# Delta-rule attention feeding an MLP: y and the new state as separate pieces, and a new written order

## The chip, the cores and the metric

The kernel runs on one core of a Trainium2 chip. The metric is the device time of one execution in microseconds, from the median of three runs. The core has a matrix engine (TensorE, PE in the profile; its weight loads stand as PEld), three engines for element-wise work (VectorE or DVE, ScalarE or ACT, GpSimd or POOL), and SyncE (SP), which issues most transfers. Each engine works through its own instructions in order and waits on semaphores for the others.

## The reference, cut to what matters

```python
def _attn_ref(q, k, v, beta):                    # (4, 8, 768, 48) each, beta (4, 8, 768)
    k_n = k / (np.linalg.norm(k, axis=-1, keepdims=True) + 1e-06)
    state = zeros((B, H, D, D)); y = zeros_like(q)
    for t in range(S):
        kt, vt, bt = k_n[:, :, t], v[:, :, t], beta[:, :, t, None]
        y[:, :, t] = einsum('bhd,bhde->bhe', q[:, :, t], state)
        v_old = einsum('bhde,bhd->bhe', state, kt)
        state = state + bt[:, :, :, None] * einsum('bhd,bhe->bhde', kt, vt - v_old)
    return y

x = y.transpose(0, 2, 1, 3).reshape(3072, 384)
h = x @ w_in                                     # (384, 2048)
g = h * np.tanh(softplus(h))
out = g @ w_out                                  # (2048, 384)
```

All values are 32-bit floats; the two weights come as 64-bit floats, read as pairs of 32-bit words.

## The kernel before, in words

The 768 time steps are cut into NS = 12 chunks of 64 (n below), and the 32 heads into two halves h of 8 pairs of heads. Within a chunk the recurrence is a triangular system. It is solved for two chunks at once (group g covers chunks 2g and 2g+1) by `early` (L1363): TensorE makes k·k products (`pg`), VectorE transposes them into `gt` (L1421), goes through some 30 dependent steps of a product `pr` (L1467) and a sum into `gt` (L1469), scales (L1471) and transposes back into `d` (L1489). Group 0 is split in halves that are put together by `merge`.

Per chunk and half TensorE then makes these small products, all in plain 32-bit float, which take two matmuls and two weight loads each: `s_a` (`ta`) and `s_b` (`tb`) apply the solve to the masked products, `s_gq` (`gq`) multiplies keys with the old state and the queries, `s_z` (`pz`) gives the corrected values, and `s_y` (L1713) gives both the transposed output y (`py`) and the new state (`ps`). In `s_y` a head's 48 state columns are written as a piece of 32 and one of 16, because the helper `new_state` lays four pieces next to each other in the array's columns (hh = 0 and 1, two pieces each). The evictions of `ps` and `py` are one deferred piece `out`, which also issues the next chunk's keys and queries (`load_k`, `load_q`) and copies the new state into `xx` on ScalarE (L1735), and the output into `x`, as a high part on ScalarE (L1740) and a low part on VectorE (L1741).

The MLP works on a chunk's 256 rows in 8 units fp of 256 hidden columns. `g1` (L1786) makes `h` from `x` (18 matmuls, two terms of high and low parts), ScalarE applies Mish into `e` (L1801) and rounds it into the high part of `g` (L1802), VectorE forms the low part (L1803), and `g2` (L1820) adds 12 matmuls into `acc`. `acc` has one pair of PSUM tiles for all chunks, copied out by ScalarE when a chunk's 8 units are in. The weights are turned from 64-bit into high and low parts in the first part of the run (`convert`, pieces `cv`, on VectorE, ScalarE, TensorE and transfers issued by GpSimd). `keep_warm` runs products of zeros while TensorE would have nothing else.

The order of all engines is written out by hand. Every piece of work is an event with a name; `put` gives it its place from the table TT (a number that sorts a priority queue), and work that a piece defers (`defer`) is an event of its own, named after it with `.0>1` and so on. An event whose `need` labels are not given yet is put back. A second table, SLOT, says which of a pool's buffers a tile gets. `tile.manual_schedule` keeps the order in which the code then issues instructions on all five engines.

The lines that the change and the prediction touch:

```python
        def new_state():                                             # in s_y
            for p in range(PB):
                for hh in (1, 0):
                    for e, m in ((0, 32), (32, D - 32)):
                        r0 = 64 * (1 - hh) + e
                        yield ps[r0:r0 + m, p, :], x[:, p, hh, D + C + e:D + C + e + m], x[:, p, hh, 0:D]
```

Of the kernel before, what the change touches and what calls it, by code (L numbers as in the profile page):

```python
# [10 lines left out]
F32 = mybir.dt.float32  # L11
# [4 lines left out]
ALU = mybir.AluOpType  # L16
# [13 lines left out]
def bcast_in(ap, n):  # L30
# [18 lines left out]
    'loadv': [13],
    'turn_k(1,0).0>1': [14],  # L50
    'loado1': [15],
    'turn_k(0,0).0>1': [16],
    'early0': [17, 25, 27, 40, 49, 51, 52, 55, 58, 59, 61, 63, 64, 65, 68, 80, 82, 84, 92, 93, 96, 97, 100, 103, 104, 105, 107, 109, 110, 120, 121, 122, 125, 127, 129, 318, 482],
    'turn_k(0,1)': [18],
    'loadq': [19],
    'cv0': [20, 28, 31, 39, 117, 136, 144, 162, 1426],
    'turn_k(0,1).0>1': [21],
    'loadb': [22],
    'warm12.401': [24],
    'loado2': [26],  # L60
    'early0.0>1': [29],
    'warm43.6': [30],
    'loado0': [32],
    'early0.1>1': [33],
    'loado11': [34],
    'loado4': [35],
    'loadi4': [37],
    'turn_k(1,1).0>1': [38],
    'turn_beta()': [41],
    'warm36.4': [42],  # L70
    'early0.2>1': [43],
    'warm11.7': [44],
    'warm0.602': [45],
    'turn_q0(0,)': [47],
    'early0.3>1': [48],
    'cv3': [50, 149, 205, 209, 213, 237, 253, 269, 1263],
    'turn_q0(1,)': [53],
    'turn_q0(0,).0>1': [54],
    'scale_v(0,0)': [56],
    'turn_q0(0,).0>2': [57],  # L80
    'cv5': [60, 108, 145, 173, 197, 208, 225, 233, 1141],
    'warm11.501': [62],
    'warm29.5': [66],
    'warm11.6': [67],
    'warm11.602': [69],
# [48 lines left out]
    'loado8': [147],
# [1950 lines left out]
```

## Time and profile before

| what | value |
|---|---|
| median of 3 runs | 640.11 us (634.57 to 641.02) |
| the profiled execution's own time | 635.71 us |
| its span, first to last instruction | 634.0 us |
| TensorE busy | 601.8 us (95%), 11118 matmuls |
| TensorE weight loads busy | 557.0 us (88%), 11118 loads |
| VectorE busy | 381.3 us (60%) |
| ScalarE busy | 280.2 us (44%) |
| GpSimd busy | 79.7 us (13%) |
| mean granted clock of TensorE | 0.982 |
| moved by transfers | 43.39 MB, mean 68 GB/s |

The span is 1.7 us shorter than the execution's own time. Busy time is the union of an engine's instructions, so a TensorE that is busy need not be at its peak: small products overlap in the array. A group's "idle before" is the time for which its engine did nothing just before an instruction of the group, with what ended the idle time; "issue" means that the engine waited for nothing that the profile shows. [...]

### The profile page before, as it was taken

To read this page: it belongs to the slowest core of one execution; us is meant where nothing else is said; L and a number is where in the kernel's file an instruction comes from. 1 tells how busy PE (TensorE), PEld (TensorE's weight loads), DVE (VectorE), ACT (ScalarE), POOL (GpSimd) and SP (SyncE) were. 2 spreads that over 40 slices of the span, in tenths; PEclk is the share of its full clock that TensorE was granted. 3 is DMA by queue.
4 is the path that set the end of the run, shared out by engine and by line. 5 is a ranking of instruction groups with operands and counts; after the bars stand their busy time and mean duration, and the time that the engine had idled before them with its cause. 6 is when DMAs were issued, how large, how long until landed. Compare 5 with 4: busy or idle time off the path is not lost.

```text
span 634.0 us, 24961 instructions
## 1 busy us (share of the span) xinstructions
PE 601.8 (95%) x11118; PEld 557.0 (88%) x11118; DVE 381.3 (60%) x837; ACT 280.2 (44%) x531; POOL 79.7 (13%) x134
## 2 busy tenths in 40 slices
PE   7989879999999889999999998999999999999997
PEld 4546668899989789899998998999999999999996
DVE  3768778998696699965847745683653432321110
ACT  3338758645433354435342533443433344343231
POOL 5100223224100040000400020210030200000000
PEclk9899989999999989999999997999999999999999
DMA  9995567932433134214231213122112312010011
GB/s 190 309 321 124 95 128 123 164 51 53 61 53 65 23 52 61 50 18 74 53 59 28 53 23 56 41 38 51 29 26 53 52 28 44 9 27 1 1 26 25
DMA packets 161818, 43.39 MB, mean 68 GB/s; under 512 B 149008, under 2 KB 157712, under 8 KB 161712
## 3 DMA queue, kind: packets, MB, share of 16 engines
q1 hardware_dynamic: 156800, 37.12, 29.6%
q0 software_dynamic: 2736, 4.20, 4.0%
q8 instruction: 87, 1.43, 0.9%
q10 hardware_dynamic: 2176, 0.49, 0.4%
q14 instruction: 19, 0.16, 0.1%
HBM read 32.87 MB, written 4.72 MB: 59 GB/s over the span
## 4 chain that ended last, share of the span: by engine, by line
PE 74%; DVE 8%; DMA 7%; issue 4%; SPq 4%; ACT 2%; POOL 0%; DVEq 0%; POOLq 0%; ACTq 0%
PE acc L1820 27%; PE h L1786 26%; SPq L1206 4%; PE py L1599 4%; PE pz L1599 3%; PE gq L1599 3%; PE pg L1406 3%; PE ps L1599 2%; DMA wi<-mi 1%; DMA xx<-in_q_dram 1%; DVE g L1803 1%; DVE pr L1467 1%; DVE gt L1469 1%; DMA ri<-in_moe_w_in_dram 1%; PE warm L1846 1%
## 5 line engine op out<-in xcount | busy, mean ns | idle before, releaser
L1820 PE MATMUL acc<-wo,g 128*128 128x384 f32 x1152 | 218.3, 342 | 2.9 <-DVE g L1803 2.8
L1786 PE MATMUL h<-x,wi 128*128 128x256 f32 x1728 | 218.9, 283 | 1.3 <-DMA wi<-mi 1.0
L1786 PEld LDWEIGHTS h<-x,wi 128*128 128x128 f32 x1728 | 212.7, 190 | 3.3 <-DMA wi<-mi 1.2
L1820 PEld LDWEIGHTS acc<-wo,g 128*128 128x128 f32 x1152 | 199.3, 189 | 6.5 <-DVE g L1803 4.4
L1803 DVE TENSOR_TENSOR g<-e,g 128x512 fp32r<-128x512 f32 x96 | 67.7, 710 | 78.4 <-ACT g L1802 74.8
L1801 ACT ACTIVATE e<-h 128x512 f32<-128x512 f32 x96 | 57.2, 598 | 119.1 <-PE h L1786 72.8
L1802 ACT CAST g<-e 128x512 fp32r<-128x512 f32 x96 | 59.1, 620 | 74.8 <-PE acc L1820 72.7
L1469 DVE TENSOR_TENSOR gt<-gt,pr 128x58 f32<-128x58 f32 (+9 forms) x164 | 58.3, 355 | 4.0
L1467 DVE TENSOR_TENSOR pr<-gt 128x58 f32<-128x58 f32 (+9 forms) x164 | 57.4, 350 | 4.1
L1599 PE MATMUL gq<-xx,kt 48*64 48x112 f32 (+1 forms) x768 | 49.4, 270 | 0.7 <-DVE xx L1584 0.6
L1599 PEld LDWEIGHTS pz<-vt,tt 64*64 64x64 f32 x768 | 43.4, 135 | 5.2 <-issue 1.5
L1599 PE MATMUL pz<-vt,tt 64*64 64x48 f32 x768 | 47.1, 226 | 0.5 <-ACT tt L1664 0.4
L1599 PEld LDWEIGHTS gq<-xx,kt 48*64 48x64 f32 x768 | 44.1, 132 | 2.6 <-issue 1.5
L1584 DVE STREAM_TRANSPOSE xx<-xx 128x1024 f32<-128x1024 f32 x20 | 24.8, 1242 | 29.9 <-DMA xx<-in_q_dram 16.9
L1577 POOL TENSOR_TENSOR vt<-vt,ne 128x384 f32<-128x384 f32 x24 | 22.1, 927 | 147.0 <-DMA vt<-in_v_dram 73.7
L1688 DVE TENSOR_TENSOR xx<-gq,amask 64x256 f32<-64x256 f32 x96 | 40.1, 418 | 0.7
L1741 DVE TENSOR_TENSOR x<-py,x 128x384 fp32r<-128x384 f32 x24 | 13.3, 556 | 44.0 <-ACT x L1740 43.8
L1406 PE MATMUL pg<-kt 48*32 48x64 f32 x1536 | 29.3, 223 | 8.6 <-issue 6.9
L1508 POOL COPY tt<-d 32x512 f32<-32x512 f32 x40 | 26.8, 669 | 83.3 <-DVE d L1489 55.9
L1406 PEld LDWEIGHTS pg<-kt 48*32 48x32 f32 x1536 | 25.6, 111 | 13.1 <-issue 8.2
L1710 ACT COPY xx<-pz 64x384 f32<-64x384 f32 x48 | 22.8, 474 | 31.3 <-PE gq L1599 11.5
L1685 DVE TENSOR_TENSOR vt<-vt,gq 128x192 f32<-128x192 f32 x44 | 15.5, 352 | 26.1 <-PE gq L1599 17.2
(135 smaller groups left out, 577.2 us busy)
## 6 DMA issues: line engine op xcount, KB each, us to landing
ri<-in_moe_w_in_dram SPq DMA_DIRECT2D x24, 256.0 KB, 5.1
ro<-in_moe_w_out_dram SPq DMA_DIRECT2D x32, 192.0 KB, 4.9
kt<-in_k_dram SPq DMA_DIRECT2D x76, 64.0 KB, 2.7
vt<-in_v_dram SPq DMA_DIRECT2D x48, 96.0 KB, 3.1
xx<-in_k_dram SPq DMA_DIRECT2D x48, 96.0 KB, 3.2
out_dram<-o SPq DMA_DIRECT2D x48, 96.0 KB, 2.2
xx<-in_q_dram SPq DMA_DIRECT2D x80, 32.0 KB, 2.4
wo<-mo POOLq DMA_DIRECT2D x9, 192.0 KB, 4.1
```

What stands on the lines that cost most here:

```text
L1206: m = (nc.scalar if turns[0] else nc.sync).dma_start(out=dst, in_=src)
L1406: nc.tensor.matmul(ps[r0:r0 + 32, p8, :], kt[r, p, c, :], mv, start=True, stop=True)
L1467: nc.vector.tensor_tensor(out=pv, in0=nj, in1=xj, op=ALU.mult)
L1469: nc.vector.tensor_tensor(out=below, in0=below, in1=pv, op=ALU.add)
L1508: nc.gpsimd.tensor_copy(out=tt2[r, t2, :, c0:c0 + 32], in_=dts[g][r, t2])
L1599: last[:] = [nc.tensor.matmul(*a, start=True, stop=True)]
L1688: nc.vector.tensor_tensor(out=x[r, p4, hh, D:D + C], in0=ps[r, :, d:], in1=bcast_mid(amask[r], 4), op=ALU.mult)
L1786: nc.tensor.matmul(h[:, f2, :], wt["i", f * P // WI * NCH + c][:, i2, f0:f0 + P], x[:, c, :], start=(i == 0), stop=(i == 3 * NCH - 1))
L1801: for d, f in ((0.7, lambda: nc.scalar.activation(e, h, AF.Mish)), (0.7, lambda: nc.scalar.copy(out=gg[:, 0], in_=e)), (0.8, lambda: nc.ve ...
L1802: (0.7, lambda: nc.scalar.copy(out=gg[:, 0], in_=e)),
L1803: (0.8, lambda: nc.vector.tensor_tensor(out=gg[:, 1], in0=e, in1=gg[:, 0], op=ALU.subtract))):
L1820: nc.tensor.matmul(acc[t], gg[:, a, f2, ts_], wt["o", f][:, i2, :], start=(f == 0 and i == 0), stop=(f == NF - 1 and i == 2))
```

## The change

The new state is a stage of its own, `s_s`, with an event, an eviction and a PSUM tile of its own. Its products take all 48 columns of a head in one piece, so a chunk and half has 16 of them in place of 32. The keys of the next chunk are issued with the state's eviction, the queries with y's; the turned queries need y's eviction only (label R), the state's eviction gives label Y. An event of `s_s` stands behind each of `s_y`. Both tables are written anew: TT has other numbers for all events, SLOT other buffers. Two lines of TT as an example (y of chunk 2, half 0):

```diff
-    'ats_y[2,0]': [630],
-    'ats_y[2,0].0>1': [631],
+    'ats_y[2,0]': [639],
+    'ats_y[2,0].0>1': [640],
+    'ats_s[2,0]': [641],
```

The code:

```diff
@@ -1722,45 +1762,44 @@
         if n not in xs:
             xs[n] = [mp.tile([P, NCH, UT], F32R, tag=f"x{i}{n % 2}", name=f"x{i}_{n}", bufs=1) for i in range(2)]
         py = placed(pa, "pa", 4, [P, NCH, 2, C], F32, f"py{n}_{h}")
-        ps = placed(pa, "pa", 4, [P, PB, D], F32, f"ps{n}_{h}") if n < NS - 1 else None
-
-        def out():
-            def state():
-                if n < NS - 1:
-                    load_k(n + 1, h)
-                    if n:
-                        load_q(n + 1, h)
-                    for hh in range(2):
-                        r = slice(64 * (1 - hh), 64 * (1 - hh) + D)
-                        nc.scalar.copy(out=x[r, :, hh, 0:D], in_=ps[r])
-
-            def result():
-                hi, lo = (t[:, :, h * P:(h + 1) * P] for t in xs[n])
-                y = py.rearrange("r c q t -> r c (q t)")
-                nc.scalar.copy(out=hi, in_=y)
-                nc.vector.tensor_tensor(out=lo, in0=y, in1=hi, op=ALU.subtract)
-                give(f"X{n}.{h}")
-
-            for f in (result, state) if h or not n else (state, result):
-                f()
-
-        def turned_y(hh):
-            cols = lambda p, a, b: flat[:, (2 * p + hh) * W + a:(2 * p + hh) * W + b]
-            pieces = [(p, e, 32) for p in range(PB) for e in ((-16, 16) if p % 2 else (0,))] + [(p, 32, 16) for p in range(0, PB, 2)]
+
+        def result():
+            hi, lo = (t[:, :, h * P:(h + 1) * P] for t in xs[n])
+            y = py.rearrange("r c q t -> r c (q t)")
+            nc.scalar.copy(out=hi, in_=y)
+            nc.vector.tensor_tensor(out=lo, in0=y, in1=hi, op=ALU.subtract)
+            give(f"X{n}.{h}")
+            if 0 < n < NS - 1:
+                load_q(n + 1, h)
+
+        cols = lambda p, hh, a, b: flat[:, (2 * p + hh) * W + a:(2 * p + hh) * W + b]
+        pieces = [(p, e, 32) for p in range(PB) for e in ((-16, 16) if p % 2 else (0,))] + [(p, 32, 16) for p in range(0, PB, 2)]
+        todo = []
+        for hh in range(2):
             for p, e, m in pieces:
                 c, r0 = divmod(D * p + e, P)
-                yield py[r0:r0 + m, c, hh, :], cols(p, e, e + m), x[:, p, hh, D:D + C]
-
-        def new_state():
-            for p in range(PB):
-                for hh in (1, 0):
-                    for e, m in ((0, 32), (32, D - 32)):
-                        r0 = 64 * (1 - hh) + e
-                        yield ps[r0:r0 + m, p, :], x[:, p, hh, D + C + e:D + C + e + m], x[:, p, hh, 0:D]
-
-        todo = [*turned_y(0), *turned_y(1), *(new_state() if n < NS - 1 else ())]
+                todo.append((py[r0:r0 + m, c, hh, :], cols(p, hh, e, e + m), x[:, p, hh, D:D + C]))
         for i, a in enumerate(todo):
-            yield mm(*a, then=(lambda: defer(2.1, out, label=f"Y{n}{h}")) if i == len(todo) - 1 else None)
+            yield mm(*a, then=(lambda: defer(2.1, result, label=f"R{n}{h}")) if i == len(todo) - 1 else None)
+
+    def s_s(n, h):
+
+        x = xx[h]
+        ps = placed(pa, "pa", 4, [P, PB, D], F32, f"ps{n}_{h}")
+
+        def state():
+            load_k(n + 1, h)
+            for hh in range(2):
+                r = slice(64 * (1 - hh), 64 * (1 - hh) + D)
+                nc.scalar.copy(out=x[r, :, hh, 0:D], in_=ps[r])
+
+        todo = []
+        for p in range(PB):
+            for hh in (1, 0):
+                r0 = 64 * (1 - hh)
+                todo.append((ps[r0:r0 + D, p, :], x[:, p, hh, D + C:D + C + D], x[:, p, hh, 0:D]))
+        for i, a in enumerate(todo):
+            yield mm(*a, then=(lambda: defer(2.1, state, need=(f"y{n}{h}",), label=f"Y{n}{h}")) if i == len(todo) - 1 else None)
 
 
     def moe(n):
@@ -1918,9 +1957,10 @@
     asks = {s_a: lambda n, h=None: [f"d{n}.{i}" for i in range(2)] + ([f"M{n}.1" if n < 2 * FG else f"D{n}" if n % 2 else f"T{n // 2}"]),
             s_b: lambda n, h=None: [f"A{n}" if h is None else f"A{n}.{h}", f"N{n // 2}" if n >= 2 * FG else f"M{n}.1"], s_gq: Q,
             s_z: lambda n, h: [f"B{n}" if n else f"B{n}.{h}", f"V{n}{h}"] + ([f"D{n}"] if n >= 2 * FG else []) + [f"G{n}{h}{i}" for i in range(2 if n else 0)],
+            s_s: lambda n, h: ([f"U{h}", "x0"] if n == 0 else []) + [f"Z{n}{h}"],
             s_y: lambda n, h: ([f"U{h}", "x0"] if n == 0 else []) + [f"Z{n}{h}"] + [f"G{n}{h}{i}" for i in range(2)]}
 
-    took = {s_a: 1.2, s_b: 1.2, s_gq: 1.1, s_z: 1.1, s_y: 1.9}
+    took = {s_a: 1.2, s_b: 1.2, s_gq: 1.1, s_z: 1.1, s_y: 1.1, s_s: 0.9}
 
     def at(t, *stages):
         def run():
@@ -1928,7 +1968,7 @@
             tensor(sum(took[f] for f, _ in todo))
             together(*(f(*a) for f, a in todo))
             for f, a in todo:
-                if f in (s_z, s_y):
+                if f in (s_z, s_y, s_s):
                     give(f"{f.__name__[2]}{a[0]}{a[1]}")
 
         want = [x for f, *a in stages if a[0] < NS for x in asks[f](*a)]
@@ -1962,6 +2002,8 @@
             put("gq00", one(together, s_gq(0, h)), TN['gq0'][h], need=Q(0, h))
     for t, st in zip((TN['st'][0], *TN['st'][:2], *TN['st'][1:]), ((s_a, 0, 0), (s_a, 0, 1), (s_b, 0, 0), (s_b, 0, 1), (s_z, 0, 0), (s_z, 0, 1), (s_y, 0, 0), (s_y, 0, 1))):
         at(t, st)
+        if st[0] is s_y:
+            at(t, (s_s, *st[1:]))
 
     put(f"early{1}", early(1), *TN['e1'], *spread(us(1 + TN['s1'][0]), us(1 + TN['s1'][1]) + 10, 60), *(us(1 + TN['s1'][1]) + 11 + i for i in range(4)), need=("K2",))
 
@@ -2009,14 +2051,18 @@
         one_a, one_b = ([(f, n + 1)] * fused(n + 1) for f in (s_a, s_b))
         at(ts[0], (s_z, n, 0), (s_gq, n, 1), *one_a)
         at(ts[1], (s_y, n, 0))
+        if n < NS - 1:
+            at(ts[1], (s_s, n, 0))
         if n == 1:
             at(ts[2], (s_z, n, 1))
             at(us(TN['g20']), (s_gq, 2, 0))
         else:
             at(ts[2], (s_z, n, 1), (s_gq, n + 1, 0), *one_b)
         at(ts[3], (s_y, n, 1))
+        if n < NS - 1:
+            at(ts[3], (s_s, n, 1))
         for h, t in ((0, us(TN['c0'] if n == 1 else TN['g20'] if n == 2 else n - 2 + (TN['c2'] if n == 3 else TN['cc'])[2])), (1, ts[0])):
-            do(t - TN['tl'], turn_q, n, h, need=(f"L{n}{h}", f"Y{n - 1}{h}"))
+            do(t - TN['tl'], turn_q, n, h, need=(f"L{n}{h}", f"R{n - 1}{h}"))
             do(t - 5.0, scale_v, n, h, need=(f"P{n}", f"ne{n // 2}"))
     at(us(TN['ab'][0]), (s_a, 1))
     at(us(TN['ab'][1]), (s_b, 1))
```

What this does to TensorE's order is seen where products of y, of the state and of a later solve meet. Before, in the run of chunk 4's last MLP units (`acc_4`), the last state pieces of 32 and 16 columns are followed at once by the 64 `pg` products, then by `acc`:

```order
L1599 MATMUL ps_0_5893<-xx_104 32x48
L1599 MATMUL ps_0_5893<-xx_104 16x48
L1406 MATMUL pg_0_5963<-kt_5783 32x64 x32
L1406 MATMUL pg_1_5998<-kt_5783 32x64 x32
L1820 MATMUL acc_4_5580<-wo_2058,g_5_5476 128x384 x3
L1820 MATMUL acc_4_5580<-wo_2131,g_5_5476 128x384 x3
L1820 MATMUL acc_4_5581<-wo_2058,g_5_5476 128x384 x3
L1820 MATMUL acc_4_5581<-wo_2131,g_5_5476 128x384 x3
```

In the changed kernel the same half of a chunk ends with 16 state products of 48 columns, and an MLP product follows:

```order
L1639 MATMUL py_0_5706<-xx_104 32x64 x12
L1639 MATMUL py_0_5706<-xx_104 16x64 x4
L1639 MATMUL ps_0_5745<-xx_104 48x48 x16
L1825 MATMUL h_0_5762<-x_5_4965,wi_735 128x256
L1825 MATMUL h_0_5762<-x_5_4966,wi_735 128x256
```

and its `pg` products stand two MLP units later:

```order
L1859 MATMUL acc_4_5132<-wo_2359,g_6_5677 128x384 x3
L1859 MATMUL acc_4_5132<-wo_2265,g_6_5677 128x384 x3
L1859 MATMUL acc_4_5133<-wo_2359,g_6_5677 128x384 x3
L1859 MATMUL acc_4_5133<-wo_2265,g_6_5677 128x384 x3
L1446 MATMUL pg_0_5804<-kt_5626 32x64 x32
L1446 MATMUL pg_1_5837<-kt_5626 32x64 x32
L1825 MATMUL h_2_5874<-x_5_4965,wi_1206 128x256
```

The `pg` products have moved away from `py` and `ps`; MLP products with 2 instructions each stand between the small ones with 4.

On VectorE the end of the solve for chunks 4 and 5 is the second place. Before, the low part of chunk 3's output (`x_3`, from `py_1`) stands ahead of the last two instructions of the solve:

```order
L1467 TENSOR_TENSOR pr_30_3889<-gt_2779 128x30
L1469 TENSOR_TENSOR gt_2779<-gt_2779,pr_30_3889 128x30
L1741 TENSOR_TENSOR x_3_3573<-py_1_3904,x_3_3572 128x3x128
L1471 TENSOR_TENSOR gt_2779<-gt_2779,y_2783 128x1024
L1489 STREAM_TRANSPOSE d_1907<-gt_2779 128x32x32
L1685 TENSOR_TENSOR vt_0_3506<-vt_0_3506,gq_01_3867 128x192
```

Now the solve ends without it; that `x_3` comes right behind these rows:

```order
L1507 TENSOR_TENSOR pr_29_3805<-gt_2807 128x58
L1509 TENSOR_TENSOR gt_2807<-gt_2807,pr_29_3805 128x2x29
L1507 TENSOR_TENSOR pr_30_3808<-gt_2807 128x30
L1509 TENSOR_TENSOR gt_2807<-gt_2807,pr_30_3808 128x30
L1511 TENSOR_TENSOR gt_2807<-gt_2807,y_2811 128x1024
L1529 STREAM_TRANSPOSE d_1778<-gt_2807 128x32x32
L1770 TENSOR_TENSOR x_3_3417<-py_1_3771,x_3_3416 128x3x128
```

The instruction that needs TensorE's `py_1` has moved behind the transposition into `d`.

In the written order the start is another one, too. Chunk 0's keys are turned before chunk 1's, behind 19 products of zeros in place of 8, and beta is loaded first on ScalarE's queue; 12 of the zero products stand ahead of the product that turns beta. Queries and values of chunk 0 are loaded behind more of the weights.

## Rows read from the trace of the kernel before

**Rows 1.** The page, part 1: busy time of each engine, share of the span, instructions.

```profile
PE 601.8 (95%) x11118; PEld 557.0 (88%) x11118; DVE 381.3 (60%) x837; ACT 280.2 (44%) x531; POOL 79.7 (13%) x134
```

**Rows 2.** Groups of TensorE by line and shape, 76.7 to 634 us; columns as titled.

```profile
line engine op names shapes xcount | busy us, mean ns | idle before us <-releasers
...
L1406 PE MATMUL pg<-kt 48*32 48x64 f32 x1280 | 25.1, 225 | 7.0 <-issue 6.9
...
L1599 PE MATMUL ps<-xx 128*16 128x48 f32 x640 | 17.6, 206 | 0.2 <-issue 0.2
L1599 PE MATMUL ps<-xx 128*32 128x48 f32 x640 | 17.6, 206 | 3.5 <-issue 3.5
```

**Rows 3.** Windows cut inside the waits called issue; counts in brackets.

```profile
core 0: us, PE busy (x) PEld busy (x) DVE busy (x) ACT busy (x) POOL busy (x), PEclk, DMA share, GB/s
...
64.90:68.90 4.00, 3.13 (x127) 2.18 (x127) 3.89 (x10) 2.80 (x6) 0.00 (x0) 1.00 0.33 58
...
72.80:88.30 15.50, 12.16 (x379) 9.96 (x380) 12.24 (x26) 11.67 (x21) 4.34 (x6) 1.00 0.85 161
...
98.50:179.50 81.00, 77.52 (x1521) 73.10 (x1521) 70.05 (x158) 47.60 (x90) 20.50 (x31) 1.00 0.51 84
```

**Rows 4.** The page, part 3: the queue that brings instructions.

```profile
q8 instruction: 87, 1.43, 0.9%
```

**Rows 5.** Windows, each some 256 TensorE instructions long and ended by a wait.

```profile
176.16:179.70 3.54, 2.20 (x142) 1.96 (x132) 3.05 (x9) 2.28 (x6) 0.00 (x0) 1.00 0.22 42
...
382.41:386.66 4.25, 2.19 (x144) 1.95 (x132) 1.91 (x4) 0.00 (x0) 0.00 (x0) 0.95 0.52 96
```

**Rows 6.** Timeline of TensorE, 308.5 to 313 us: start, length, what.

```profile
308.64 1.10 PE L1599 MATMUL py<-xx 128*32 128x64 f32 x64
309.56 0.86 PE L1599 MATMUL ps<-xx 128*32 128x48 f32 x64
310.35 2.35 PE L1820 MATMUL acc<-wo,g 128*128 128x384 f32 x12
```

**Rows 7.** Timeline of TensorE, start-up: products of 64 columns, two abreast.

```profile
59.15 1.14 PE L1599 MATMUL pz<-vt,tt 64*64 64x48 f32 x32 [0.42 <-ACT tt L1664]
```

**Rows 8.** Windows with a lowered granted clock (column PEclk).

```profile
88.60:93.00 4.40, 4.40 (x32) 4.10 (x31) 2.76 (x6) 1.32 (x3) 0.00 (x0) 0.61 0.35 64
...
386.60:393.20 6.60, 6.55 (x111) 6.38 (x112) 3.33 (x5) 3.01 (x6) 0.00 (x0) 0.51 0.34 49
225.80:229.30 3.50, 3.50 (x27) 3.45 (x20) 2.98 (x3) 2.16 (x4) 0.83 (x2) 0.51 0.25 35
```

**Rows 9.** Timeline of VectorE, end of the solve for chunks 4 and 5.

```profile
219.97 0.56 DVE L1741 TENSOR_TENSOR x<-py,x 128x384 fp32r<-128x384 f32 x1 [4.65 <-ACT x L1740]
220.44 1.22 DVE L1471 TENSOR_TENSOR gt<-gt,y 128x1024 f32<-128x1024 f32 x1
221.70 1.98 DVE L1489 STREAM_TRANSPOSE d<-gt 128x1024 f32<-128x1024 f32 x1
```

**Rows 10.** Timeline of TensorE: the product that waits for it.

```profile
224.77 1.21 PE L1599 MATMUL ta<-d,at 32*32 32x32 f32 x64 [2.02 <-DVE xx L1688]
```

**Rows 11.** Windows: the solve for chunks 2 and 3.

```profile
99.40:146.30 46.90, 44.97 (x562) 42.36 (x560) 44.14 (x105) 29.07 (x55) 11.51 (x16) 1.00 0.65 105
```

**Rows 12.** The page, part 5: what lies between a first and a second MLP product.

```profile
L1803 DVE TENSOR_TENSOR g<-e,g 128x512 fp32r<-128x512 f32 x96 | 67.7, 710 | 78.4 <-ACT g L1802 74.8
L1801 ACT ACTIVATE e<-h 128x512 f32<-128x512 f32 x96 | 57.2, 598 | 119.1 <-PE h L1786 72.8
L1802 ACT CAST g<-e 128x512 fp32r<-128x512 f32 x96 | 59.1, 620 | 74.8 <-PE acc L1820 72.7
```

**Rows 13.** Timeline of TensorE: the first MLP product on TensorE.

```profile
76.70 2.37 PE L1786 MATMUL h<-x,wi 128*128 128x256 f32 x18
```

**Rows 14.** Timeline of VectorE, start-up.

```profile
20.86 0.36 DVE L1265 TENSOR_SCALAR ro<-ro 128x384 f32<-128x384 f32 x1 [2.48 <-DMA ro<-in_moe_w_out_dram]
```

**Rows 15.** Who waited for whom, total, times, longest.

```profile
DVE g L1803 <- ACT g L1802: 74.8, 31, 8.9
```

More of the change, by code (lines that the diff above doesn't have):

```diff
@@ L54 @@
[L54 to L73, printed above, removed]
@@ new lines @@
+    'merge0.2>1': [187],
+    'merge0.3>1': [190],
+    'ats_a[0,0]': [191],
+    'ats_a[0,0].0>1': [192],
+    'loado9': [193],
+    'ats_a[0,1]': [195],
+    'ats_a[0,1].0>1': [197],
+    'loado10': [200],
+    'merge1': [201, 229, 246, 286],
+    'cv22': [203, 204, 237, 262, 455, 480, 486, 487, 502],
+    'warm12.301': [205],
+    'warm40.201': [206],
+    'unit(0,)': [207],
+    'ats_b[0,0]': [211],
+    'ats_b[0,1]': [213],
+    'warm11.801': [214],
+    'cv15': [215, 219, 239, 346, 347, 348, 349, 354, 1227],
@@ new lines @@
+    'ats_gq[0,1].0>1': [217],
+    'cv13': [224, 315, 336, 367, 368, 369, 371, 381, 920],
+    'ats_b[0,0].0>1': [225],
+    'ats_b[0,1].0>1': [227],
+    'merge1.1>1': [230],
+    'merge1.0>1': [232],
+    'ats_z[0,0]': [233],
+    'ats_z[0,0].0>1': [234],
+    'ats_z[0,1]': [235],
+    'loadx': [236],
+    'cv21': [243, 301, 302, 340, 434, 460, 461, 462, 463],
+    'unit(1,)': [247],
+    'loadi5': [250],
+    'cv9': [251, 260, 261, 276, 284, 291, 292, 293, 438],
+    'loadp': [252],
+    'scale_v(1,0)': [253],
@@ new lines @@
+    'g1.2.0': [703],
+    'g1.2.0.0>1': [704],
+    'g1.2.1': [705],
+    'ats_y[3,0]': [706],
+    'g1.2.1.0>1': [707],
+    'g1.2.1.0>2': [708],
+    'early3.2>1': [709],
+    'ats_s[3,0]': [712],
+    'g2.1.7': [721],
+    'ats_y[3,0].0>1': [723],
+    'prep(4,)': [728],
+    'g2.1.7.0>1': [731],
+    'scale_v(4,1)': [732],
+    'g1.2.0.0>2': [733],
+    'g1.2.0.0>3': [734],
+    'g1.2.1.0>3': [739],
+    'g1.2.2': [740],
+    'g1.2.2.0>1': [741],
+    'turn_q(4,0)': [742],
+    'early3.6>1': [745],
@@ new lines @@
+    'g2.2.2': [782],
+    'g1.2.5': [784],
+    'g1.2.5.0>1': [786],
+    'g1.2.5.0>2': [787],
+    'g1.2.5.0>3': [788],
+    'ats_a[4].0>1': [789],
+    'g2.2.3': [790],
+    'g2.2.4': [791],
+    'turn_q(4,1)': [796],
+    'prep(5,)': [797],
+    'g1.2.6': [798],
+    'g1.2.6.0>1': [799],
+    'g1.2.7.0>2': [800],
+    'g1.2.7.0>3': [801],
+    'g1.2.6.0>2': [802],
+    'g1.2.6.0>3': [803],
+    'ats_b[4]': [804],
+    'ats_s[3,1]': [805],
+    'ats_b[4].0>1': [806],
+    'g1.3.1': [807],
+    'scale_v(5,0)': [808],
@@ L959 @@
+    'g2.11.6': [1592],
+    'g2.11.7': [1593],
+    'g2.11.7.0>1': [1594],
+    'g2.11.7.0>2': [1595],
 }
 SLOT = {
[72 rows of a table removed]
[68 rows of a table added]
 }
```

1688 lines of the change are left out of this document (813 added, 875 removed), and 187 rows, old and new, of tables (SLOT, TT).

## The prediction

> **What bounds the kernel now.** I read the page's first part first. TensorE is busy 601.8 us, 95% of the span; VectorE 60%, ScalarE 44% [rows 1]. So from the first MLP product at 76.7 us [rows 13] to the end the time is TensorE's work, its few pauses, and what a lowered clock costs. The groups of TensorE name the pauses: of all small products after 76.7 us, `pg` waited 7.0 us and `ps` 3.7 us, and nearly all of both, 6.9 + 3.5 + 0.2 = 10.6 us, is put down to "issue", a wait for nothing that the profile shows [rows 2].
>
> What is that wait? I cut windows at the places where it occurs and counted matmuls and weight loads between them: 254, 759 and 3042 [rows 3]. These are 1, 3 and 12 times 256, short by about 1%. The queue that brings instructions moved 1.43 MB in 87 packets, 16.4 KB each, and 87 times 256 is 22,272, against the 22,236 matmuls and loads that TensorE has [rows 1, 4]. So I read the pauses as TensorE waiting for its own instructions, which come in blocks of 256. The stretches that end in such a pause are short ones: about 270 instructions in 3.54 and 4.25 us, with 1.3 and 2.1 us of it idle [rows 5]. They are places where `py`, `ps` and `pg` stand back to back. A small fp32 product takes four instructions and little time: 64 `py` records and 64 `ps` records pass in 1.71 us, where 12 `acc` records alone take some 2.3 [rows 6].
>
> [...]
>
> **The change, part by part.** The sum starts from the profiled execution's own time, 635.7 us.
>
> *State products in pieces of 48 columns.* 64 records become 32 per chunk and half, 22 times. That is half the instructions, but not half the time: before, four pieces lie beside each other in the array, and 64 records pass in 0.79 us (`ps` at 309.56, `acc` at 310.35) [rows 6], 16 sets of four. The 32 new ones stand two abreast, again 16 sets, each with the same 48 columns to stream. I take the same time, 0. Bounds: half the time if instructions were what counts, -0.40 × 22 = -8.7. Above, the nearest row with two abreast: 32 records of `pz` last 1.14 us, 64 of `ps` 0.86 [rows 6, 7], +0.28 × 22 = +6.1. The two ends are far apart, and the middle is supported by streaming alone.
>
> Where `py` gives way to `ps` nothing pauses before: the two overlap in the records [rows 6]. [...]
>
> *Pauses for instructions.* Some 700 matmuls and as many loads go, and above all the written order no longer puts `pg` behind `py` and `ps`; MLP products stand between them, which give the queue time. A block of 256 took about 3.3 us to arrive when the engine outran it (3.54 us for 274 instructions in the first of rows 5). In the new order the runs of small products without MLP work between them are shorter than two blocks in all but a couple of places. -10.6, and I leave 1.5 for those: -9.1. Ends: -10.6 and 0.
>
> *Clock behind those pauses.* The first two stretches of rows 8 follow pauses of this kind. They cost (1 - 0.61) × 4.4 = 1.7 and (1 - 0.51) × 6.6 = 3.2 us. If the pause goes, so does the stretch: -4.9. Ends: -4.9 and 0.
>
> *The wait of `ta` for chunk 4.* In the new order the low part of `x` is behind the transposition, so the solve's end no longer waits for `py`: -2.0 [rows 10], and with it its clock stretch, (1 - 0.51) × 3.5 = -1.7 [rows 8]. What is late next is `ta` of chunk 2. VectorE is 44.14 of 46.90 us busy in that solve [rows 11]: what TensorE saves up to there it has to wait for, unless VectorE gains too, by 2.8 us at the most. I count +3 for that, ends 0 and +6.
>
> *Start-up.* The order of loads is new, and so are the 19 products of zeros. Up to 76.7 us one pause for instructions lies at 64.9 to 68.9, where TensorE is busy 3.13 of 4.00 us [rows 3], and VectorE waits 2.48 us for a weight's load [rows 14]. I take -2 for the first MLP product. Ends: both waits gone and as much again by an earlier solve, -6; a load that comes as late as that one does now, +2.5.
>
> *Evictions.* The state's ScalarE copies and `y`'s are now two events, and the keys of the next chunk are issued with the one, the queries with the other. The number of instructions on ScalarE and VectorE is the same, and both have idle time, so 0; the cover is ScalarE's 56% of idle time [rows 1].
>
> *New close neighbours.* Between the first and second MLP product of a unit stand 0.60, 0.62 and 0.71 us, 1.93 in all, without the handovers [rows 12]. In the new order a second product follows its first at about 2 us of TensorE's work in three places, and `acc` of one chunk follows the copy of the last one directly in two. Each may cost up to its 1.93 us less what stands between: +3 in all, ends 0 and 5 × 1.6 = +8.
>
> Sum: 635.7 + 0 - 9.1 - 4.9 - 2.0 - 1.7 + 3 - 2 + 3 = 622.0 us for an execution like the profiled one. That execution lies 4.4 us under the median of the runs, 640.1, and 1.1 above the fastest of them, 634.6. The mean of the four times that I have (634.6, 635.7, 640.1, 641.0) is 637.9, 2.1 above the profiled one. I add these 2 us and forecast 624, 2.5% under the median before. I take 1% as what a measurement can tell from no change here.
>
> For its own range I take the root of the squares of the terms' half widths, about 7.4 (state products), 5 (pauses), 2.5 (clock), 3 (VectorE), 4 (start-up) and 4 (neighbours): 11 us to either side, 613 to 635.
>
> **Rivals.**
>
> *The pauses stay.* The "issue" waits could be something else than instructions on their way, or the blocks could fall as badly in the new order. For it: nothing in the trace names the cause. Against: the counts in rows 3. Then 9.1 and 4.9 us are not gained: 624 + 14 = 638, no change by the 1% bound. [...]
>
> *The wide pieces don't run abreast.* A piece of 48 columns reaches over the places of two of the old pieces. If two such can't be in the array at the same time, 32 sets take the place of 16, each 0.79/16 = 0.049 us: +0.79 × 22 = +17, so 641: no change. For it: no row shows this shape. Against: `pz` has 32 records of 64 rows and 64 columns, which last 1.14 us with its tail, less than the 32 × 0.049 = 1.57 of as many single ones [rows 7].
>
> *VectorE's queue, the slower side.* The new order interleaves low parts of `g` and the solve's steps anew. VectorE works in order, so a low part of `g` that is written too early holds all solve steps behind it until ScalarE's rounding, which waits for TensorE's `h`. Such waits are there now: 31 times, 74.8 us, the longest 8.9 [rows 15]. Where VectorE has slack they cost nothing. In a solve that is 94% busy [rows 11] one of the longest kind would delay `d` by up to 8.9 us, and TensorE, which has to have `ta`, with it. From 640 + 6.4 us on it is slower, so from 22.4 us over the forecast: three such waits, one in each of three solves, 624 + 3 × 8.9 = 651. For it: the wait of 4.65 us in rows 9 is just of this kind. Against: the mean of the 31 is 2.4 us, and of the later solves' time most is not that tight (VectorE is 60% busy in all).
>
> **How the numbers follow.** Forecast 624: 0.74. The pauses stay, 638: 0.09. Not abreast, 641: 0.08. VectorE's queue, 651: 0.09. Faster by over 1% is under 633.7: the forecast's share but for its uppermost part, and the first rival with luck in the other terms, 0.74 together. Slower by over 1% is above 646.5: 0.09. In between: 0.17. The range 611 to 638 takes in the forecast's own and the first rival's time; the second and the third lie outside.
>
> **What would show it.** Right: in the groups of TensorE after the first MLP product, idle time by "issue" of at most 2 us; 32 `ps` records of 48 columns in about 0.8 us from the first to what follows; no stretch at a clock of 0.5 after 80 us; the first `h` near 74; `ta` of chunk 4 without a wait; instruction packets down from 87 to some 81. Wrong: issue waits of the old size in other places (then the blocks were not understood); `ps` at 1.1 us or more (the pieces' width); TensorE idle behind VectorE in 100 to 225 us (the solve's queue); waits of `acc` for ScalarE by more than 5 us (the neighbours). The most likely error of the sum is the state products, whose bounds lie 15 us apart.

## The result and the profile after

The changed kernel takes 613.18 us in the median of 4 runs (612.22 to 614.96), the kernel before 637.34 us in its now 4 runs; the ratio is 0.963 with a 95% interval of 0.955 to 0.971. The forecast was 624, range 611 to 638. So the direction and the range held, and the gain is about half as large again as forecast (24 us against 16).

The page's first part and the queue that brings instructions, of the changed kernel (execution of 612.22 us, span 610.5; to compare with [rows 1, 4]):

```profile
PE 593.7 (97%) x10414; PEld 549.7 (90%) x10414; DVE 380.1 (62%) x837; ACT 282.1 (46%) x532; POOL 78.2 (13%) x134
...
q8 instruction: 82, 1.34, 0.9%
```

704 matmuls and as many loads fewer, and five packets of instructions fewer. TensorE's busy time fell by 8 us only; the span by 23.5. The rest was idle time. The groups of TensorE from the first MLP product on (to compare with [rows 2]; same columns):

```profile
L1825 PE MATMUL h<-x,wi 128*128 128x256 f32 x1728 | 215.7, 281 | 0.6 <-ACT e L1840 0.6
L1859 PE MATMUL acc<-wo,g 128*128 128x384 f32 x1152 | 214.5, 339 | 0.0
L1639 PE MATMUL gq<-xx,kt 48*64 48x112 f32 x672 | 45.5, 275 | 1.9 <-issue 1.5 <-DVE xx L1624 0.3
...
L1639 PE MATMUL py<-xx 128*32 128x64 f32 x1056 | 21.7, 221 | 0.5 <-ACT xx L1750 0.5
L1446 PE MATMUL pg<-kt 48*32 48x64 f32 x1280 | 20.4, 217 | 1.2 <-issue 1.2
L1639 PE MATMUL ps<-xx 128*48 128x48 f32 x640 | 18.3, 210 | 0.0
```

"issue" is down from 10.6 to 2.7 us. Added up over all groups, TensorE idles 4.2 us after its first MLP product, before 17.7; waits for VectorE are 0.3 us, before 5.4. Two more windows show the clock and the counts between two pauses that are left (columns as in [rows 3]):

```profile
core 0: us, PE busy (x) PEld busy (x) DVE busy (x) ACT busy (x) POOL busy (x), PEclk, DMA share, GB/s
...
88.60:93.00 4.40, 4.40 (x88) 4.07 (x86) 4.16 (x10) 4.15 (x7) 0.00 (x0) 1.00 0.25 42
...
86.90:422.70 335.80, 332.85 (x6207) 319.31 (x6207) 260.57 (x572) 160.59 (x298) 49.88 (x80) 1.00 0.35 59
```

In the window where the clock (PEclk, the granted share of the full one) was 0.61 before [rows 8] it is 1.00, and in the 336 us after it too. Between the pauses at 86.9 and 422.8 us stand 12,414 instructions of the two kinds: 49 times 256 is 12,544, again short by 1%, as in [rows 3]. So what is left of the pauses falls on the same grid.

The first MLP product, its time before being 76.70 [rows 13], and a `py` and `ps` stretch (to compare with [rows 6]):

```profile
74.13 2.36 PE L1825 MATMUL h<-x,wi 128*128 128x256 f32 x18
...
288.36 1.10 PE L1639 MATMUL py<-xx 128*32 128x64 f32 x64
289.39 0.92 PE L1639 MATMUL ps<-xx 128*48 128x48 f32 x32
290.25 2.35 PE L1859 MATMUL acc<-wo,g 128*128 128x384 f32 x12
```

From `ps` to the next it is 0.86 us in place of 0.79, and from `py` to `ps` 1.03 in place of 0.92: 32 wide products take 0.18 us more with their neighbours than 64 narrow ones; one at a time they would have taken 0.79 us more by the estimate in the rival on the wide pieces, so they run two abreast. Last, `ta` of chunk 4 and VectorE's work for it (to compare with [rows 9, 10]):

```profile
201.54 1.10 PE L1639 MATMUL py<-xx 128*32 128x64 f32 x64
202.57 1.20 PE L1639 MATMUL ta<-d,at 32*32 32x32 f32 x64
```

```profile
198.63 1.23 DVE L1511 TENSOR_TENSOR gt<-gt,y 128x1024 f32<-128x1024 f32 x1
199.90 2.06 DVE L1529 STREAM_TRANSPOSE d<-gt 128x1024 f32<-128x1024 f32 x1
203.23 0.56 DVE L1770 TENSOR_TENSOR x<-py,x 128x384 fp32r<-128x384 f32 x1 [1.28 <-ACT x L1769]
```

`d` is there at 201.96, 0.6 us ahead of `ta`, which waits for nothing.

### The profile page after: what moved, and what is told of

It is laid out like the page before. It is cut to its first block, busy times and chain, and to the rows that moved or that the text cites. A ratio compares the mean times of both kernels' runs of the same rounds, so it can differ in the third digit from the quotient of the medians.

```text
span 610.5 us, 23544 instructions
## 1 busy us (share of the span) xinstructions
PE 593.7 (97%) x10414; PEld 549.7 (90%) x10414; DVE 380.1 (62%) x837; ACT 282.1 (46%) x532; POOL 78.2 (13%) x134
## 4 chain that ended last, share of the span: by engine, by line
PE 77%; DVE 7%; DMA 6%; ACT 4%; SPq 3%; issue 2%; DVEq 0%; ACTq 0%
PE acc L1859 30%; PE h L1825 28%; PE py L1639 4%; DMA ro<-in_moe_w_out_dram 4%; SPq L1246 3%; PE pz L1639 3%; PE gq L1639 3%; PE ps L1639 3%; PE pg L1446 2%; DMA vt<-in_v_dram 2%; DVE gt L1509 2%; DVE pr L1507 1%; DVE g L1842 1%; PE tb L1654 1%; PE ta L1654 1%
## 5 line engine op out<-in xcount | busy, mean ns | idle before, releaser
L1825 PE MATMUL h<-x,wi 128*128 128x256 f32 x1728 | 215.7, 281 | 0.6 <-ACT e L1840 0.6
L1859 PE MATMUL acc<-wo,g 128*128 128x384 f32 x1152 | 214.5, 339 | 0.0
L1825 PEld LDWEIGHTS h<-x,wi 128*128 128x128 f32 x1728 | 208.5, 188 | 2.9 <-ACT e L1840 0.8
L1859 PEld LDWEIGHTS acc<-wo,g 128*128 128x128 f32 x1152 | 197.9, 188 | 2.7 <-DVE g L1842 0.4
L1507 DVE TENSOR_TENSOR pr<-gt 128x58 f32<-128x58 f32 (+9 forms) x164 | 54.4, 332 | 4.0
L1750 ACT COPY xx<-pz 64x384 f32<-64x384 f32 x48 | 22.7, 473 | 38.6 <-PE gq L1639 14.8
L1885 PE MATMUL warm<-zero 128*128 128x512 bf16 x107 | 28.0, 412 | 1.5 <-DVE zero L1195 1.5
L1446 PEld LDWEIGHTS pg<-kt 48*32 48x32 f32 x1536 | 22.4, 107 | 6.3 <-issue 4.0
L1446 PE MATMUL pg<-kt 48*32 48x64 f32 x1536 | 24.7, 217 | 3.3 <-issue 2.6
(136 smaller groups left out, 563.9 us busy)
```

What stands on the lines that cost most here:

```text
L1446: nc.tensor.matmul(ps[r0:r0 + 32, p8, :], kt[r, p, c, :], mv, start=True, stop=True)
L1507: nc.vector.tensor_tensor(out=pv, in0=nj, in1=xj, op=ALU.mult)
L1825: nc.tensor.matmul(h[:, f2, :], wt["i", f * P // WI * NCH + c][:, i2, f0:f0 + P], x[:, c, :], start=(i == 0), stop=(i == 3 * NCH - 1))
L1859: nc.tensor.matmul(acc[t], gg[:, a, f2, ts_], wt["o", f][:, i2, :], start=(f == 0 and i == 0), stop=(f == NF - 1 and i == 2))
L1885: nc.tensor.matmul(warm, zb[:, 0:P], zb[:, :512], start=True, stop=True)
```

## The experiments

The kernels' times have a start-up in them that varies (the first MLP product comes between 72.5 and 80.4 us in the kernels of the changed order), so each is also read from its first MLP product (`h`) to the end of its span. "Idle" and "issue" are added up over TensorE's groups in that part. In the row of `before_xlo` the columns that are read from a profile are left empty, since its profiled execution, of 640.8 us, lies 5.9 us above its median:

| kernel | median us | ratio to before (95%) | first `h` | from there to the end | idle | of it issue |
|---|---|---|---|---|---|---|
| before | 637.3 | 1 | 76.7 | 557.3 | 17.7 | 10.6 |
| changed | 613.2 | 0.963 (0.955–0.971) | 74.1 | 536.4 | 4.2 | 2.7 |
| changed, again | 613.7 | 0.965 (0.960–0.970) | 79.9 | 536.1 | 4.7 | 3.1 |
| after_ps32 | 621.9 | 0.976 (0.971–0.982) | 80.4 | 536.7 | 6.0 | 3.4 |
| before_ps48 | 636.0 | 1.001 (0.996–1.005) | 79.0 | 552.6 | 15.3 | 4.6 |
| after_shift48 | 615.9 | 0.967 (0.962–0.972) | 75.5 | 539.0 | 5.4 | 3.8 |
| after_shift144 | 609.5 | 0.957 (0.952–0.963) | 73.2 | 535.1 | 3.2 | 1.1 |
| after_shift144, again | 609.4 | 0.960 (0.956–0.964) | 72.5 | 534.8 | 3.2 | 0.6 |
| after_first152 | 613.2 | 0.965 (0.961–0.968) | 76.1 | 533.8 | 2.4 | 0.8 |
| after_xlo | 622.4 | 0.979 (0.973–0.985) | 74.6 | 542.0 | 7.4 | 1.2 |
| before_pgapart | 632.0 | 0.994 (0.991–0.998) | 76.8 | 554.4 | 17.9 | 5.7 |
| before_xlo | 635.0 | 0.995 (0.990–1.000) | – | – | – | – |
| before_apart_xlo | 632.0 | 0.994 (0.991–0.997) | 78.7 | 550.7 | 15.1 | 5.7 |
| before_shift156 | 645.5 | 1.016 (1.011–1.020) | 81.5 | 563.9 | 21.6 | 12.5 |

### The pieces alone, both ways

The state's pieces undone in the changed kernel:

```diff
-                todo.append((ps[r0:r0 + D, p, :], x[:, p, hh, D + C:D + C + D], x[:, p, hh, 0:D]))
+                for e, m in ((0, 32), (32, D - 32)):
+                    todo.append((ps[r0 + e:r0 + e + m, p, :], x[:, p, hh, D + C + e:D + C + e + m], x[:, p, hh, 0:D]))
```

> The changed kernel with the state's products back in pieces of 32 and 16 columns (64 records per chunk and half), order and places as changed; 1408 more TensorE instructions. Theory (instruction blocks): the pauses called issue after the first MLP product come back in part, 5 to 9 us in all against 2.8 now, at other places than in the kernel before (by counting 256 instructions per block: near 94, 147, 185, 198, 223 and 341 us of the changed kernel's time), one or two stretches of the lower clock with them (1.7 us each), while the py and ps stretches get some 2.8 us shorter, as they were before the change: 615 to 620 us. Rival 1 (the wide pieces are the whole gain, by fewer records): about 630 to 637 us. Rival 2 (the order alone is the gain and the pauses belong to the code's places, not to counts): issue stays under 3 us and the shorter stretches give 610 us.

Measured 621.9 us. From the first `h` to the end it is 536.7 us, the same as the changed kernel: 0.7 us more issue, not 2 to 6, and shorter `py` and `ps` stretches against it. The places of the pauses (197.9, 233.7, 237.5, 288.8 us) met the expected list at one point only. In the profile the loss lies ahead of the first `h`, 80.4 us against 74.1, where a pause of 2.96 us stands at 74.7 us and long products follow it (32 `gq` in 3.25 us, in `before_ps48` 1.75). No row shows the clock of that stretch; over the whole execution the granted clock is 0.982, in the changed kernel 0.992. But the changed kernel run again had its first `h` at 79.9 too, with a median of 613.7, so a single profile does not settle why the median is 8 us up. Both rivals fell: neither 630 nor 610. The theory's own sizes fell as well: it had 615 to 620 us and 5 to 9 us of issue, and 621.9 and 3.4 us came.

And the wide pieces alone in the kernel before:

```diff
-                    for e, m in ((0, 32), (32, D - 32)):
-                        r0 = 64 * (1 - hh) + e
-                        yield ps[r0:r0 + m, p, :], x[:, p, hh, D + C + e:D + C + e + m], x[:, p, hh, 0:D]
+                    r0 = 64 * (1 - hh)
+                    yield ps[r0:r0 + D, p, :], x[:, p, hh, D + C:D + C + D], x[:, p, hh, 0:D]
```

> The kernel before with only the state's products made 48 columns wide, its own order and buffers. Theory (instruction blocks): 1408 instructions fewer, the back-to-back stretches are 448 instead of 512 instructions; issue after the first MLP product falls from 10.6 to 4 to 9 us, at 170, 205, 254, 282, 325 us and so on, the ps and py stretches cost some 2.8 us more; time 2 to 8 us under before (ratio 0.987 to 0.997). Rival 1 (the pieces are the whole gain): ratio near 0.963. Rival 2 (the order is all): ratio 1.00 to 1.005, issue unchanged at 10 us.

The ratio is 1.001 (0.996 to 1.005), no difference, although issue did fall to 4.6 us. TensorE's groups tell where a part of it went (two of them, from the first `h` on):

```profile
L1406 PE MATMUL pg<-kt 48*32 48x64 f32 x1280 | 22.0, 217 | 5.5 <-issue 2.8 <-ACT at L1415 1.6 <-DVE xx L1688 1.1
...
L1599 PE MATMUL ps<-xx 128*48 128x48 f32 x640 | 18.5, 210 | 0.0
```

6.0 us of issue went, and 3.6 us of other idle time came (among it ScalarE's `at` and VectorE's `xx`); longer `py` and `ps` stretches took another part. This does not account for the equal medians: in the profiled execution, of 633.3 us, the part behind the first `h` is 4.7 us shorter than before and the start-up 2.3 us longer. Why the medians are the same stays open. The longer stretches are the pieces' own doing, since the order is that of before:

```profile
308.59 1.10 PE L1599 MATMUL py<-xx 128*32 128x64 f32 x64
309.62 0.92 PE L1599 MATMUL ps<-xx 128*48 128x48 f32 x32
310.48 2.35 PE L1819 MATMUL acc<-wo,g 128*128 128x384 f32 x12
```

The same 1.03 and 0.86 us as in the changed kernel. So the pieces by themselves bring nothing in the old order. The new order without them (`after_ps32`) brings 15 of the 24 us, and the pieces some 8 us of the median on top of it; where those 8 us lie is not shown. "Order" takes in all the rest of the change: no run separates the two evictions or the new loads at the start from it.

### Are the pauses instructions on their way?

The test is to add instructions that do nothing and stand ahead of everything. Products of zeros were cut into three, with the same 512 columns in all:

```diff
+    made = iter(range(1000))
...
         for _ in range(n):
-            nc.tensor.matmul(warm, zb[:, 0:P], zb[:, :512], start=True, stop=True)
+            cuts = (0, 171, 342, 512) if 19 <= next(made) < 31 else (0, 512)
+            for a, b in zip(cuts, cuts[1:]):
+                nc.tensor.matmul(warm[:, a:b], zb[:, 0:P], zb[:, a:b], start=True, stop=True)
```

> The changed kernel in which 12 of the products of zeros near 17 us are cut into three each (171, 171 and 170 columns, the same 512 columns in all): 48 TensorE instructions more, ahead of everything that follows, nothing else changed. Theory (instruction blocks): all later block boundaries move by 48 instructions, so the pauses move: the one of 1.5 us at 423 us goes, and new ones of about 1 to 1.5 us stand near 101, 251, 354, 464 and 551 us, 4.6 to 9 us in all after the first MLP product, with some lowered clock: 617 to 625 us. Rival (pauses belong to places in the code, or come from transfers): the pause at 423 us stays, no others, 613 us.

The pause at 423 us went, and others came at 109.8, 153.2, 263.3, 475.3 and 563.1 us. The expected times had been read from the trace with its pauses taken out, so some 9 to 12 us are to be added to them, which was seen only afterwards: four of the five are there (101, 251, 464, 551), the one at 354 isn't, and that at 153 was not on the list. The sizes were overestimated: 1.8, 1.4, 0.1, 0.4 and 0.1 us, 3.8 us of issue in all with one of 0.25 us at 82.6, and 615.9 us. The first of them and the windows between pauses:

```profile
107.53 0.44 PE L1859 MATMUL acc<-wo,g 128*128 128x384 f32 x1
109.79 1.69 PE L1859 MATMUL acc<-wo,g 128*128 128x384 f32 x6 [1.82 <-issue]
```

```profile
82.60:109.78 27.18, 25.36 (x635) 23.80 (x635) 25.19 (x62) 25.90 (x51) 7.91 (x11) 1.00 0.80 136
109.78:153.15 43.37, 41.93 (x633) 40.31 (x633) 37.21 (x82) 21.67 (x40) 14.41 (x21) 0.96 0.42 71
263.30:475.30 212.00, 211.07 (x3675) 204.12 (x3676) 133.66 (x281) 89.35 (x165) 22.76 (x39) 1.00 0.25 43
```

The pause now stands in the middle of an `acc` run, behind its first product, an instruction that never waited so before. The windows hold 1,270 and 1,266 instructions (5 times 256 is 1,280), and 7,351 (29 times 256 is 7,424). A pause that belonged to `pg` or to a data transfer would not keep that count.

The traces hold more. TensorE also has instructions that are neither matmul nor weight load, 207 for semaphores and 3 drains in the kernel before; they are the 1% by which the counts fall short. Counted with them, all 121 waits called issue of 0.15 us or more, in the 14 profiles, stand at instruction 256k + 194 or 256k + 195, with k a whole number. The packets of the instruction queue are recorded too, 16,384 bytes each: every one of the 121 waits ends 1.1 to 1.7 us after packet k landed, and at each of the 1,179 places 256k + 194 at most one further packet had landed. In the kernel before it was none at 70 of the 87 places and one at 17, in the changed one none at 68 of 82 and one at 14. I read this as TensorE waiting there for its next 256 instructions.

Why the order matters shows in the same count. Behind the first `h`, TensorE worked through 9 of 75 blocks of the kernel before in under 3 us (the issue wait not counted), and 7 of these ended in such a wait. In the changed kernel it was 2 of 70, and one of them waited.

With 36 products cut (144 instructions more, `31` becomes `55`):

> As the one with 48 more instructions, but 36 products of zeros cut into three: 144 more. Theory (instruction blocks): by the same count hardly a boundary falls into a dense stretch after the first MLP product: issue there 0 to 0.5 us in place of 2.8; in the start-up the pause of 3.1 us at 41.6 us (boundary in the mb products) goes too; 608 to 612 us. Rival (places or transfers): the pauses at 41.6 and 423 us stay, 613 us or some more for the extra instructions.

609.5 us, as expected, with 1.1 us of issue behind the first `h` in place of 0 to 0.5. The pause in the `mb` products did not go as expected: it is 1.1 us long and ends at 44.0 us. Beside the changed kernel on one chip it is 609.4 against 613.7 us:

> The kernel with 144 more instructions in the start-up again, beside the changed kernel: 2 to 4 us under it (pauses of 3.1 us at 41.6 and 1.5 us at 423 us gone). Rival (chance of one chip): the same as the changed kernel.

> The changed kernel as it is, for a comparison on the same chip with the two that follow: ratio to before 0.963.

The pause of 1.5 us at 423 us is gone and 0.6 to 1.1 us of issue are left behind the first `h`. The time is lower by 4 us in both comparisons, though the two intervals still overlap. Behind the first `h` the profiles differ by 1.3 us only; the rest would lie in the start-up, which varies. In the repeat the `mb` pause is 1.6 us, beside 3.3 us in the changed kernel's. This is the fastest version that was run.

The first 19 products of zeros cut into five each:

> The changed kernel with its first 19 products of zeros cut into five each: 152 TensorE instructions more, ahead of everything else. Theory (instruction blocks): block boundaries after the first MLP product as harmless as with 144 (0 to 1 us of issue there), and the second block's fetch starts earlier, so that the pause of 1.4 to 2 us at 15.7 us shrinks too: 606 to 610 us, 3 to 6 us under the changed kernel. Rival: the first solve isn't what the start-up waits for, or the slower products of zeros delay the first keys: no better than 144, 609 to 611 us.

613.2 us, no better than with 144, as the rival has it, and above the rival's 609 to 611. From the first `h` on it is the best of all (533.8 us), but the start-up lost 2 to 4 us: TensorE paused 2.2 us at 12.7 and 1.0 at 18.4 us, both in `pg`. More instructions in front only moved the boundaries: in the start-up two of them now cause a pause in `pg`, where the changed kernel has one, at 15.6 us.

And in the kernel before, 39 products cut into three, so that the count is another one:

> The kernel before with 39 products of zeros from 10 us on cut into three: 156 instructions more. Theory (instruction blocks): in the order before, no count is good: issue after the first MLP product 12 to 18 us in place of 10.7, at more and other places; time from 0 to 7 us longer, since in that order waits for VectorE and ScalarE stand behind the pauses and shrink as these grow: ratio 1.00 to 1.01. Rival (the kernel before merely had an unlucky count, the changed one a lucky one): issue falls by half, ratio 0.985 or less.

1.016, above the 1.00 to 1.01 expected, with 12.5 us of issue behind the first `h` (12 to 18 expected). That the kernel before merely had an unlucky count does not fit: in its order the one other count that was run is worse.

### Parts of the order

The five pairs of `pg` moved behind the next MLP unit, in the kernel before (ten numbers of TT, two for each pair; one pair of them):

```diff
-    'early3': [..., 661, 662, ...],
+    'early3': [..., 676.1, 676.2, ...],
```

> The kernel before with five pairs of pg products (chunks 6, 8, 9, 10 and 11), which stand right behind a py and ps stretch, each moved behind the next MLP unit (12 or 18 products); pieces, buffers and everything else as before. Theory (instruction blocks): the dense stretches are broken up, issue after the first MLP product falls from 10.7 to 3.5 to 7 us (what is left: 80 to 90 us, and near 192, 237 and 285 us of the kernel before), and the clock stretch behind the pause at 386 us (3.2 us) goes: 6 to 11 us under before, ratio 0.983 to 0.991. Rival (pg waits for something of its own, or the pauses move on to the next small products undiminished): ratio 1.00, issue near 10 us.

0.994 (0.991 to 0.998), less than expected, though issue came down to 5.7 us as it should. Idle time in all is 17.9 us, as before. Two of the new waits:

```profile
305.61 0.31 PE L1599 MATMUL gq<-xx,kt 48*64 48x112 f32 x1 [2.39 <-DVE xx L1584]
...
394.44 1.79 PE L1786 MATMUL h<-x,wi 128*128 128x256 f32 x13 [1.46 <-ACT e L1801]
```

The first had been 0.3 us and the second did not exist. My reading, which no run isolates: in the order before, the pauses gave VectorE and ScalarE time; take a pause away and the next product is early for its operand. Idle time did not fall, so the 2.9 us gained behind the first `h` are something else: the mean granted clock is 0.992 in this profile and 0.982 before, and my estimate is that the clock behind one pause (3.2 us at 386 us [rows 8]) is most of it.

The swap on VectorE, in the kernel before, alone and together with these moves (`early2`'s last solve step at 779.5 in place of 782):

> The kernel before with one swap on VectorE: the last two instructions of the solve for chunks 4 and 5 (gt times y, the transposition into d) stand ahead of the low part of chunk 3's output, as in the changed kernel. Theory: ta's wait of 2.0 us at 224.8 us goes, and the lower clock behind it (1.7 us): 3.7 us less, ratio 0.994. Rival: TensorE waits for the next VectorE result instead (the masked state xx, the low part of g), ratio 1.00.

635.0 us, 0.995 (0.990 to 1.000), as expected in size, with an interval that nearly reaches 1.

> Both edits of the two kernels above together in the kernel before. Theory: the gains add, 10 to 15 us under before, ratio 0.977 to 0.985, so that more than half of what the change brings comes from these six moves with the pieces left as they were. Rival (the changed order gains by many small waits of VectorE and ScalarE that go, and not by these): ratio 0.99 or above.

0.994: the two do not add up. `ta` does not wait in it (223.21 us, without idle time in front), but idle time only fell to 15.1 us. Here the rival held: these six moves are not what the changed order gains by. That it gains by suiting all its places to each other is what is left; no run shows it.

The swap undone in the changed kernel:

```diff
-    'ats_y[3,1].0>1': [776],
+    'ats_y[3,1].0>1': [773.5],
```

> The changed kernel with that swap undone: the low part of chunk 3's output stands ahead of the last two instructions of the solve, as before the change. In the changed kernel ta stands right behind py on TensorE, so it would wait for the copy of py, the low part (0.56), gt times y (1.23) and the transposition (2.06), about 4.5 us in all, and some clock behind it (1.7 to 3.4 us): 6 to 8 us over the changed kernel, ratio to before 0.972 to 0.976. Rival: the low part's place costs TensorE nothing, ratio 0.963.

```profile
202.15 1.10 PE L1639 MATMUL py<-xx 128*32 128x64 f32 x64
207.61 1.57 PE L1639 MATMUL ta<-d,at 32*32 32x32 f32 x64 [4.36 <-DVE d L1529]
```

The wait is 4.36 us (4.5 expected), `ta` itself takes 1.57 in place of 1.20 us, 15 `h` products behind it 3.12 us where 18 ahead of it took 2.36 (no row shows the clock of this stretch), and from the first `h` on the kernel is 5.6 us longer. The ratio is 0.979 (0.973 to 0.985; 0.972 to 0.976 expected). In the new order this one place on VectorE is worth more than it was in the old one.

## Why the prediction was right, and where it was off

- **Pauses for instructions** (-9.1, ends -10.6 and 0): measured 10.6 to 2.7, -7.9. Right in mechanism and size. I had left 1.5 us for dense places, and named 2 us as the most; 2.7 are left, in `gq` and `pg`. The windows of [rows 5] are one block of 256 each; the 274 and 276 counted in them take in records that were under way at their ends.
- **Clock** (-4.9, and -1.7 behind `ta`): all three stretches are gone, -6.6, right. One of the old kind is still there in the start-up, behind a pause of 3.1 us:

```profile
41.60:48.30 6.70, 6.70 (x114) 3.90 (x115) 1.63 (x4) 1.55 (x3) 1.21 (x2) 0.50 0.90 162
```

- **`ta` of chunk 4** (-2.0): gone, and `after_xlo` shows that the place of `x`'s low part is what decides it (4.36 us of waiting with the part ahead of the solve's end, none with it behind).
- **State products** (0, bounds -8.7 and +6.1): +0.18 us at a stretch, up to +3.9 in 22 of them. They run abreast (+0.79 us at a stretch was the estimate for one at a time), so that rival is out. 0.11 us of the 0.18 lies between `py` and `ps`, in either order: 1.03 us with the wide pieces (changed, `before_ps48`), 0.92 with the narrow ones (before, `before_apart_xlo`). So it comes with the shape; its cause is not shown.
- **Limit by VectorE in the solve of chunks 2 and 3** (+3): this step failed; it came out as 0. The start and the end of that solve on VectorE, and the `ta` of chunk 2 that needs it, before and in the changed kernel:

```profile
99.39 2.08 DVE L1421 STREAM_TRANSPOSE gt<-d 128x1024 f32<-128x1024 f32 x1
144.19 2.09 DVE L1489 STREAM_TRANSPOSE d<-gt 128x1024 f32<-128x1024 f32 x1
146.33 1.20 PE L1599 MATMUL ta<-d,at 32*32 32x32 f32 x64
```

```profile
88.30 2.12 DVE L1461 STREAM_TRANSPOSE gt<-d 128x1024 f32<-128x1024 f32 x1
132.33 2.08 DVE L1529 STREAM_TRANSPOSE d<-gt 128x1024 f32<-128x1024 f32 x1
134.62 1.20 PE L1639 MATMUL ta<-d,at 32*32 32x32 f32 x64
```

  The solve is nearly as long as before, 46.1 us after 46.9, and `ta` follows it at once in both. But it starts 14.2 us behind the first `h` in place of 22.7, because the `pg` products that it needs are done at 87.6 us in place of 98.9. I read a VectorE that is 94% busy [rows 11] as one that cannot be ahead. A share of busy time bounds how long the solve takes, not when it starts.
- **Other waits for VectorE**: a term that I left out. Without the 2.0 of `ta` they went from 3.4 to 0.3 us, -3.1. Most of them were `acc` waiting for the low part of `g`; the group before:

```profile
L1820 PE MATMUL acc<-wo,g 128*128 128x384 f32 x1152 | 218.3, 342 | 2.9 <-DVE g L1803 2.8
```

- **Close neighbours** (+3): waits for ScalarE rose from 0.2 to 1.1 us, +0.9. Distances of about 2 us were nearly enough here. One wait for a transfer of weights (1.0 us) went as well.
- **`pg` itself**: a term that I left out. Its busy time fell from 25.1 to 20.4 us, -4.7, for the same 1280 records. Some 1.5 us of it is the lower clock behind the pause at 386 us (99 records in 2.98 us, at a granted clock of 0.51), which stands under clock already. What the other 3.2 us come from is not shown.
- **Start-up** (-2): -2.6 here. The repeat shows that this was chance: 79.9 us there, with three pauses of 2.2 to 3.3 us ahead of it, and the rest of the kernel the same to 0.3 us (536.4 and 536.1).
- **The median** (+2.1 over the profiled run): +1.0.

Added up: -7.9 - 6.6 - 2.0 + 3.9 - 3.1 + 0.9 - 1.0 - 4.7 - 2.6 = -23.1, of which the 1.5 us of clock within `pg` are counted twice: -21.6, against 635.71 - 612.22 = 23.5 measured, so 1.9 us stay without a name. Most of the forecast's miss of 10.8 us is the +3 that did not come, the 3.1 us of other waits for VectorE and some 3.2 us of `pg`, 9.3 us together; the other differences nearly cancel.

The rival "the pauses stay" fell with the shifts. The slower rival, VectorE's queue, did not come to pass, but `after_xlo` shows that its mechanism is real: one low part ahead of a solve's end costs 4.36 us at that place.

## What to carry to other kernels

Count instructions as well as columns. Where a stretch of small products issued 256 instructions in less than about 3 us, TensorE mostly outran them here (7 of 9 such blocks behind the first `h` of the kernel before), and a pause of 0.5 to 3.5 us followed, behind two of the long ones a lower clock (0.61 over 4.4 us and 0.51 over 6.6 us [rows 8]). Put long products between such stretches, and cut some filler products to see whether the pauses move with the count. A pause taken away alone may bring nothing, if other engines were catching up in it; look at total idle time, not at the one releaser that fell.

## What the runs showed of the hardware

- TensorE's instructions come in blocks of 256 (87 packets of 16,384 bytes for 22,446 instructions before, 82 for 21,033 in the changed kernel), and its pauses called issue stand at the same place of a block: 121 of 121 at instruction 256k + 194 or 195, each ending 1.1 to 1.7 us after packet k of the instruction queue landed. Adding 48 instructions of no use to the start took the pause of 1.55 us at 423 us away and brought one of 1.8 us at 110 us; 144 left 0.6 to 1.1 us of pauses behind the first `h`, against 2.7 and 3.1 us without them.
- Such pauses also go with the length of the start-up. In the changed kernel's two profiles three of them stand at the same instructions, 1.4, 3.1 and 0.8 us long in the first and 2.5, 3.3 and 2.2 us in the second, and the first MLP product comes 5.8 us later in the second. What of the scatter between executions that explains is open, as only one of each is profiled.
- A lower clock, 0.5, followed the pause of 3.1 us at 41.6 us in the changed kernel for 6.7 us; the pause of 1.55 us at 423 us in it was followed by none (1.00 from 422.8 to 425.8 us).
